# The opening of an attention and feed-forward kernel: the first root by logarithm and Newton step, three squares on VectorE, one copy moved

## Chip, core and metric

The kernel runs on one core of a Trainium2 chip. The metric is the time of one execution on the device in microseconds (us). Time before: 1337.54 us, the median of 3 runs (1336.25 to 1338.61). A core has a matrix engine (TensorE, PE in the profile), three engines for element-wise work (VectorE or DVE, ScalarE or ACT, GpSimd or POOL), and an engine (SP) that here does nothing but send transfers between main memory and the on-chip memory. Every engine takes its own instructions in order; they wait for one another through semaphores.

## What is computed

```python
def _attn_ref(q, k, v, g_q, g_k):            # q, k, v: (8, 12, 448, 64)
    def rmsnorm(x, g):
        rms = np.sqrt(np.mean(x * x, axis=-1, keepdims=True) + 1e-06)
        return x / rms * g
    q_n, k_n = (rmsnorm(q, g_q), rmsnorm(k, g_k))
    scores = scale * np.matmul(q_n, k_n.transpose(0, 1, 3, 2))
    attn = softmax(scores)                   # row maximum taken off, 1e-9 added to the sum
    return np.matmul(attn, v)

def _moe_ref(x, w_in, w_out):                # x: (3584, 768), w_in: (768, 2048), w_out: (2048, 768)
    r = np.maximum(x @ w_in, 0.0)
    return (r * r) @ w_out
```

Attention's output, with the heads side by side, is the `x` of the second function. All of it is in float32.

## The kernel before

Two heads of one batch row make a *pair*; there are 48. Pairs 0 to 11 (`NAT` is 12) are done first and alone, in `attention_alone`; the pairs that follow are done beside the matrix products of the feed-forward part, which come in four spans by a Strassen-like scheme with seven products in place of eight. The order of the work in each engine is the order in which the program is written (`manual_schedule`): nothing is moved by a scheduler.

**The first pair.** `first_pair` sends the loads of pair 0 and 1 (SP's queue: q(0), the two gain vectors, k(0), q(1), k(1)), fills `mhalf` with -0.5 on POOL, and has PE run three idle products on a zeroed tile. Then `normalise_in_turn` makes the roots. In the text q(i) and k(i) are the query and key halves of pair i. For each half: ACT squares it (L333), DVE adds up in groups of 64 (L334) and makes mean plus 1e-6 (L335), POOL raises that to the power -0.5 (L336). After the root of q, DVE multiplies q by it (L339), and that is the copy which PE transposes. k is not scaled: its root goes into the exponentials as a factor (L828). `between` stands after q's power: the three DVE steps for a bound on the scores (L1604 to L1606) and the product of the gains (L373). PE transposes k(0) and q(0) (L385), ACT copies both out of the PSUM banks (L387, L389, the latter with the gain).

Then all engines load the bound and branch: small scores take `attention_then_ffn_bounded`, which needs no row maximum. This is the branch that runs.

**A pair in `attention_alone`.** The 448 keys of a pair are cut into four chunks (`NJ`). `scores(i, c)` has PE make two products (one for each head) into one of two PSUM tiles `sc` (L824), and ACT takes two exponentials out of it (L828). A third chunk's products thus wait for the exponentials of the first. `transpose(i, s, n)` transposes q or k of the next pair (L794) and copies it (L796 for k, L803, in `gain`, for q). `values` multiplies by v (L887), `total_of` makes the row sums (L912), `add_up` adds chunks of exponentials on DVE (L841), `finish` turns the sums into factors and writes `xT` on DVE (L930 to L936).

`norm(i)` normalises the pair two ahead. For i up to 2 it calls `normalise_in_turn`, both squares on ACT. From i = 3 on one square takes both halves (L731), and `roots` makes the root without POOL: ACT takes a logarithm (L742) and an exponential (L743, with a bias tile `rebias`), DVE makes a Newton step of three small instructions (L744 to L746), POOL scales q (L747).

**The weights.** Beside this the weights are prepared in steps, `prepare(t)` for block t, four ticks each. The steps that the text names: ACT's absolute value (`unsigned`, L594), DVE's clamp (L608) in the first tick; ACT's scaling of the low words (L611) and DVE's shift (L613) in the second; DVE's merge (L618) in the third; POOL's integer addition of block t-1 (`value`, L580) in the third and fourth; POOL's sums and differences (L588). SP's loads of the blocks (L545) are in `load_words`. Each `yield` of `attention_alone` is a turn u, and after it `weights(upto)` runs ticks until `upto` are done:

```python
for u, _ in enumerate(attention_alone()):
    weights(min(EARLY, 2 * u + 1, 4 + (EARLY - 4) * u // (4 * NAT - 7)))
```

`EARLY` is 48. Before, 1, 3, 5, 7 and 8 ticks are done after turns 0 to 4. Pair 0 has one turn, the pairs that follow have four.

**The order in pair 0** is: scores (0,0) and (0,1), transposes of k(1), scores (0,2) and (0,3), transposes of q(1), `add_up`, `norm(2)`, load of v(1), first half of the values, load of pair 3.

Of the kernel before, what the change touches and what calls it, by code (L numbers as in the profile page):

```python
# [325 lines left out]
        nc.sync.dma_start(dst[:, :, h], k[b, h0 + h].rearrange("(p j) d -> p j d", j=4))  # L326


def normalise_in_turn(nc, raw, sq, rstd, mhalf, between=lambda: None):

    SP, _, n = rstd.shape
    for s in range(2):
        nc.scalar.activation(sq[:, s], raw[:, s], AF.Square)  # L333
        nc.vector.tensor_reduce(rstd[:, s], sq[:, s].rearrange("p (n d) -> p n d", n=n), AX, ALU.add)  # L334
        nc.vector.tensor_scalar(rstd[:, s], rstd[:, s], float(n) / sq.shape[2], 1e-6, ALU.mult, ALU.add)  # L335
        nc.gpsimd.tensor_tensor(rstd[:, s], rstd[:, s], mhalf[:SP, 0:n], ALU.pow)  # L336
        if s == 0:
            between()
            nc.vector.tensor_tensor(sq[:, 0].rearrange("p (j h d) -> p h j d", j=n // 2, h=2),  # L339
                                    raw[:, 0].rearrange("p (h j d) -> p h j d", j=n // 2, h=2),  # L340
                                    rstd[:, 0].rearrange("p (h j) -> p h j ()", h=2)
                                    .to_broadcast([SP, 2, n // 2, sq.shape[2] // n]), ALU.mult)


def chunk_of(pt, s, j, n):
# [4 lines left out]
def first_pair(tc, q, k, g_q, g_k, held):  # L350

    nc = tc.nc
    qk, qkT, ident, mhalf, gains, rstd, bound = held
    D = q.shape[-1]
    S = q.shape[2]
    NJ = 4
    SP = S // NJ
    raw, sq = (places_of(qk, 0, n)[:SP] for n in range(2))
    load_q(nc, qk, q, 0)
    bound[0]()  # L360
    load_k(nc, qk, k, 0)
    for i, g in enumerate((g_q, g_k)):
        for h in range(2):
            nc.gpsimd.dma_start(gains[h * D:(h + 1) * D, i:i + 1], g.rearrange("(d o) -> d o", o=1))
    load_q(nc, qk, q, 1)
    load_k(nc, qk, k, 1)
    nc.gpsimd.memset(mhalf, -0.5)
    make_identity(nc, ident)


    def between():
        bound[1]()
        nc.vector.tensor_scalar(gains[:, 0:1], gains[:, 0:1], gains[:, 1:2], float(D) ** -0.5, ALU.mult, ALU.mult)  # L373

    with tc.tile_pool(name="ps_first", bufs=1, space=bass.MemoryType.PSUM) as ps_first:

        nc.vector.memset(qkT[:, 1], 0.0)
        idle = ps_first.tile([2 * D, S], F32, name="idle")
        for _ in range(3):
            nc.tensor.matmul(idle, qkT[:, 1, 0, 0:2 * D], qkT[:, 1, 1], start=True, stop=True)  # L380
        normalise_in_turn(nc, raw, sq, rstd, mhalf, between)
        for s, src in ((1, raw[:, 1]), (0, sq[:, 0])):
            pt = ps_first.tile([2 * D, S], F32, name=f"pt{s}")
            for j in range(NJ):
                nc.tensor.transpose(chunk_of(pt, s, j, NJ), src[:, j * 2 * D:(j + 1) * 2 * D], ident[:SP, :SP])  # L385
            if s:
                nc.scalar.copy(qkT[:, 0, s], pt)  # L387
            else:
                nc.scalar.activation(qkT[:, 0, s], pt, AF.Copy, scale=gains[:, 0:1])  # L389
# [3 lines left out]
def attention_then_ffn_bounded(  # L393
# [73 lines left out]
        turn[0] += n is None  # L467
        return ps_m.tile([P, S], F32, tag="mn"[turn[0] % 2 if n is None else n], name=name)

    qk, qkT, ident, mhalf, gains, rstd0, _ = held  # L470
    gT = consts.tile([P, NFC, 2 * S], F32, name="gT")
    xT = consts.tile([P, 2, NPAIR, S], F32, name="xT")
    xC = consts.tile([P, 3, HC, S], F32, name="xC")
# [247 lines left out]
    def norm(i):  # L721
        if i >= NAT:
            squares(i)
            norm_by_squares(i)
            return scale_by_squares(i)
        raw, sq = (places_of(qk, i, n)[:SP] for n in range(2))
        rstd = rstds[i] = small.tile([SP, 2, 2 * NJ], F32, tag="rstd", name="rstd", bufs=4)
        normed[i] = sq[:, 0], raw[:, 1]
        if i <= 2:
            return normalise_in_turn(nc, raw, sq, rstd, mhalf)  # L730
        nc.scalar.activation(sq, raw, AF.Square)  # L731
        nc.vector.tensor_reduce(rstd, sq.rearrange("p s (n d) -> p s n d", d=D), AX, ALU.add)
        nc.vector.tensor_scalar(rstd, rstd, 1.0 / D, 1e-6, ALU.mult, ALU.add)

    def roots(i):


        raw, sq = (places_of(qk, i, n)[:SP] for n in range(2))
        rstd = rstds[i]
        flat = rstd.rearrange("p s n -> p (s n)")  # L740
        y, t = (small.tile([P, 2 * S // 32], F32, tag=tag, name=tag)[:SP, 0:4 * NJ] for tag in ("half", "other"))
        nc.scalar.activation(y, flat, AF.Ln, scale=2.0 ** -63)  # L742
        nc.scalar.activation(y, y, AF.Exp, scale=-0.5, bias=sums["rebias"])  # L743
        nc.vector.scalar_tensor_tensor(t, y, -0.5, flat, ALU.mult, ALU.mult)  # L744
        nc.vector.tensor_tensor(t, t, y, ALU.mult)
        nc.vector.scalar_tensor_tensor(flat, t, 1.5, y, ALU.add, ALU.mult)  # L746
        nc.gpsimd.tensor_tensor(sq[:, 0].rearrange("p (j h d) -> p h j d", j=NJ, h=2),  # L747
                                raw[:, 0].rearrange("p (h j d) -> p h j d", j=NJ, h=2),
                                rstd[:, 0].rearrange("p (h j) -> p h j ()", h=2).to_broadcast([SP, 2, NJ, D]),
                                ALU.mult)  # L750
# [36 lines left out]
    def transpose(i, s, n):  # L787

        if n is None:
            pt = bank("pt", 1) if i % 2 == 0 else ps_o.tile([P, S], F32, tag="o", name="pt")  # L790
        else:
            pt = bank("pt", n)
        for j in range(NJ):
            nc.tensor.transpose(chunk_of(pt, s, j, NJ), normed[i][s][:, j * P:(j + 1) * P], ident[:SP, :SP])  # L794
        if s:
            nc.scalar.copy(qkT[:, i % 2, s], pt)  # L796
        elif n is None:
            turned[i] = pt
        else:
            gain(i, pt)  # L800
# [1 line left out]
    def gain(i, pt):  # L802
        nc.scalar.activation(qkT[:, i % 2, 0], pt, AF.Copy, scale=gains[:, 0:1])  # L803

    def scores(i, c):


        if i >= NAT:
            sc = ps_s.tile([P, 2, 512], F32, tag="s", name="sc")
            n = S if c < NF else S // 2  # L810
            for h in range(2):
                rows = slice(h * D, (h + 1) * D)
                for m, part in enumerate(sides):
                    keys = slice(c * P + m * D, c * P + (m + 1) * D) if c < NF else slice(NF * P, S)
                    of = slice(0, S) if c < NF else slice(m * n, (m + 1) * n)
                    nc.tensor.matmul(sc[part, h, 0:n], qkT[rows, 0, 1, keys], qkT[rows, 0, 0, of], start=True, stop=True)  # L816
            pr = probs[i, c] = places[(NF * i + c) % len(places)] if c < NF else halves[i % 2]
            nc.scalar.activation(pr, sc[:, :, 0:n], AF.Exp)  # L818
            return
        at = i % 2  # L820
        sc = ps_s.tile([SP, 2, 512], F32, tag="s", name="sc")
        for h in range(2):
            rows = slice(h * D, (h + 1) * D)
            nc.tensor.matmul(sc[:, h, 0:S], qkT[rows, at, 1, c * SP:(c + 1) * SP], qkT[rows, at, 0, :],  # L824
                             start=True, stop=True)
        pr = probs[i, c] = places[(NJ * i + c) % len(places)][:SP]
        for h in range(2):
            nc.scalar.activation(pr[:, h], sc[:, h, 0:S], AF.Exp, scale=rstds[i][:, 1, 2 * c + h:2 * c + h + 1])  # L828
# [124 lines left out]
    def attention_alone():  # L953


        for i in range(NAT):
# [5 lines left out]
            if i == 0:  # L962

                transpose(1, 1, 1)
                scores(0, 2)
                scores(0, 3)
                transpose(1, 0, 0)
                add_up(0, 1)
                norm(2)
                load_v(1)  # L970
                values(0, (0, 1))
                load(3)
                yield
                continue
# [524 lines left out]
    with tc.tile_pool(name="words", bufs=2) as spare["pool"]:  # L1499
# [5 lines left out]
        with tc.tile_pool(name="first", bufs=2, reuse_waits="tile") as work:  # L1505
# [4 lines left out]
            sums["turned"], sums["factors"] = (g[:, 0:S] for g in free[2 * NJ + 2:2 * NJ + 4])  # L1510
            sums["ones"] = work.tile([SP, D], F32, tag="ones", name="ones", bufs=1)
            nc.vector.memset(sums["ones"], 1.0)
            sums["rebias"] = work.tile([SP, 1], F32, tag="rebias", name="rebias", bufs=1)
            nc.vector.memset(sums["rebias"], -31.5 * math.log(2.0))
            for u, _ in enumerate(attention_alone()):

                weights(min(EARLY, 2 * u + 1, 4 + (EARLY - 4) * u // (4 * NAT - 7)))
                if u == 4 * NAT - 9:
                    load_blocks(5)
        with tc.tile_pool(name="first_product", bufs=2, reuse_waits="tile") as work:  # L1520
# [54 lines left out]
def kernel(  # L1575
# [27 lines left out]
    def square_of_bound():  # L1603
        nc.vector.tensor_tensor(gg[:, 0, :], gg[:, 0, :], gg[:, 1, :], ALU.mult)  # L1604
        nc.vector.tensor_tensor(gg[:, 0, :], gg[:, 0, :], gg[:, 0, :], ALU.mult)
        nc.vector.tensor_reduce(top, gg[:, 0, :], AX, ALU.max)  # L1606

    held = (
        bound.tile([128, 8, 8 * D], F32, name="qk"),
        bound.tile([128, 2, 2, S], F32, name="qkT"),  # L1610
        bound.tile([128, 128], F32, name="ident"),
        bound.tile([128, 2 * (S // 32)], F32, name="mhalf"),
        bound.tile([128, 2], F32, name="gains"),
        bound.tile([S // 4, 2, 8], F32, name="rstd0"),
        (load_gains, square_of_bound),
    )
    with tc.manual_schedule():
# [42 lines left out]
```

## Time and profile before

| what | value |
|---|---|
| median of 3 runs | 1337.54 us (1336.25 to 1338.61) |
| the profiled execution, its own time | 1336.47 us |
| its span, from first to last instruction | 1334.6 us |
| PE busy | 1319.8 us (99%) |
| DVE, ACT, POOL busy | 856.0, 486.4, 678.7 us |
| DVE, ACT, POOL busy from 0 to 20 us | 9.68, 14.65, 12.11 us |
| PE busy from 0 to 20 us, from 20 to 57, from 57 to 60, from 60 to 127 | 16.63, 36.14, 2.65, 66.16 us |
| clock granted to PE | 1.00 in all stretches of the opening |

The page puts 93% of the chain that ended last on PE. A busy time near the length of a stretch means that the engine sets the pace there or is close to it. In a timeline each line has its start, its duration, the engine, the line of the program, the operation and its operands with their shapes; `qk<-qk` names the tile written and the tile read. Idle time before an instruction stands in brackets, with the last work that ended before it; a wait for several things is put down to the one that came last by the profile.

### The profile page before, as it was taken

What the parts mean: (1) busy time and instruction counts of PE and PEld (TensorE: products, weight loads), DVE (VectorE), ACT (ScalarE), POOL (GpSimd) and SP (SyncE); (2) the same over time, 40 slices, a digit from 0 to 9 for tenths busy, and PEclk for the clock granted to TensorE, in tenths of its full rate; (3) what the DMA queues carried; (4) which work ended last, traced back from release to release, by engine and by line L of the source; (5) the groups of instructions that cost most, each with busy time, mean ns of one, the idle gap of its engine ahead of it and who ended that gap; (6) DMA issues with size and microseconds to landing.
All of it is one profiled execution on the core that took longest, in us unless ns stands there. A gap on an engine that the chain in (4) does not pass through costs nothing.

```text
span 1334.6 us, 17767 instructions
## 1 busy us (share of the span) xinstructions
PE 1319.8 (99%) x5930; PEld 699.0 (52%) x5930; DVE 856.0 (64%) x1334; ACT 486.4 (36%) x939; POOL 678.7 (51%) x544
## 2 busy tenths in 40 slices
PE   8999999999999999999999999999999999999997
PEld 3334454444446654444444755444444665557887
DVE  6999898589987233467887523457888723336553
ACT  8885656555540012255542011235554001111000
POOL 5677444467756123566774322448775622322452
PEclk9999999999999999999999999999999999999999
DMA  8787999656664333356656433345764444321433
GB/s 233 217 219 197 361 384 324 188 125 133 138 152 117 85 89 88 99 115 140 132 130 144 100 98 89 99 109 111 140 134 126 114 90 153 115 87 48 116 106 55
DMA packets 413817, 190.18 MB, mean 142 GB/s; under 512 B 282388, under 2 KB 408724, under 8 KB 413716
## 3 DMA queue, kind: packets, MB, share of 16 engines
q1 hardware_dynamic: 406164, 180.21, 51.7%
q0 software_dynamic: 4736, 8.40, 2.5%
q8 instruction: 49, 0.80, 0.3%
q10 hardware_dynamic: 2816, 0.34, 0.2%
q14 instruction: 52, 0.43, 0.1%
HBM read 155.72 MB, written 33.16 MB: 142 GB/s over the span
## 4 chain that ended last, share of the span: by engine, by line
PE 93%; DVE 3%; ACT 2%; issue 1%; DMA 1%; POOL 0%; SPq 0%; ACTq 0%
PE ps L1217 21%; PE pd L1117 11%; PE pa L1117 10%; PE pc L1117 10%; PE sc L816 7%; PE pav L898 7%; PE pb L1117 5%; PE ps L1400 3%; PE ps L1268 3%; PE pd L1372 2%; PE pc L1372 2%; PE pa L1372 2%; PE sc L824 2%; PE pav L887 2%; PE pd L1202 1%; PE pa L1202 1%
## 5 line engine op out<-in xcount | busy, mean ns | idle before, releaser
L1089 POOL TENSOR_TENSOR gT<-gT 128x448 f32<-128x448 f32 x96 | 93.7, 978 | 258.5 <-ACT gT L1085 258.5
L773 POOL TENSOR_TENSOR half<-half,mhalf 128x28 f32<-128x28 f32 x36 | 184.7, 5131 | 68.2 <-DVE half L772 46.0
L1217 PE MATMUL ps<-gT,sw 128*128 128x448 f32 x432 | 169.3, 545 | 0.0
L1085 ACT ACTIVATE gT<-gT 128x448 f32<-128x448 f32 x96 | 55.3, 576 | 293.7 <-DVE gT L1133 293.6
L1117 PE MATMUL pa<-xT,sw 128*128 128x448 f32 x384 | 154.9, 539 | 0.0
L1217 PEld LDWEIGHTS ps<-gT,sw 128*128 128x128 f32 x432 | 80.1, 190 | 87.1 <-issue 85.3
L1217 PE MATMUL ps<-gC,sw 128*128 128x448 f32 x288 | 113.1, 546 | 0.0
L816 PE MATMUL sc<-qkT 64*64 64x448 f32 (+1 forms) x1152 | 110.0, 497 | 0.3 <-ACT pr L818 0.2
L1117 PEld LDWEIGHTS pa<-xT,sw 128*128 128x128 f32 x384 | 72.8, 190 | 70.7 <-issue 70.7
L588 POOL TENSOR_TENSOR gC<-gC 128x384 f32<-128x384 f32 x64 | 72.1, 1144 | 60.2 <-DVE gC L584 58.5
L1217 PEld LDWEIGHTS ps<-gC,sw 128*128 128x128 f32 x288 | 53.3, 190 | 59.5 <-issue 58.2
L866 POOL DMA_DIRECT2D xT<-factors x72 | 38.0, 532 | 90.9 <-DMA factors<-square 59.0
L1133 DVE TENSOR_TENSOR gT<-z,pd 128x448 f32<-128x448 f32 x32 | 19.9, 621 | 99.1 <-PE pd L1117 98.9
L818 ACT ACTIVATE pr<-sc 128x896 f32<-128x896 f32 x87 | 76.9, 908 | 12.0 <-PE sc L816 11.8
L775 POOL TENSOR_TENSOR qk<-qk,half 128x448 f32<-128x448 f32 x72 | 76.7, 1085 | 2.8
L1117 PE MATMUL pd<-xT,sw 128*128 128x448 f32 x192 | 77.8, 541 | 0.2
L1117 PE MATMUL pd<-xC,sw 128*128 128x448 f32 x192 | 77.5, 540 | 0.0
L1117 PE MATMUL pc<-xC,sw 128*128 128x448 f32 x192 | 77.5, 540 | 0.0
L1117 PE MATMUL pc<-xT,sw 128*128 128x448 f32 x192 | 77.4, 539 | 0.0
L1117 PE MATMUL pb<-xC,sw 128*128 128x448 f32 x192 | 77.4, 539 | 0.0
L898 PE MATMUL pav<-pr,vt 64*64 64x448 f32 x348 | 72.7, 537 | 0.0
L898 PE MATMUL rest<-pr,vt 64*64 64x448 f32 x348 | 72.7, 537 | 0.0
(282 smaller groups left out, 2447.6 us busy)
## 6 DMA issues: line engine op xcount, KB each, us to landing
sw<-w1s SPq DMA_DIRECT2D x224, 192.0 KB, 2.4
sw<-w2s SPq DMA_DIRECT2D x102, 256.0 KB, 3.4
w1s<-gC SPq DMA_DIRECT2D x8, 1344.0 KB, 7.3
w2s<-gC SPq DMA_DIRECT2D x8, 1344.0 KB, 6.3
qk<-in_q_dram SPq DMA_DIRECT2D x144, 56.0 KB, 2.5
qk<-in_k_dram SPq DMA_DIRECT2D x144, 56.0 KB, 2.5
xT<-factors POOLq DMA_DIRECT2D x72, 112.0 KB, 3.5
words<-in_moe_w_out_dram SPq DMA_DIRECT2D x9, 768.0 KB, 7.5
```

Source lines behind the costliest of these rows:

```text
L588: nc.gpsimd.tensor_tensor(*[blocks_of(n)[:, place_of(n, i)] for i in (dst, x, y)], op)
L773: nc.gpsimd.tensor_tensor(half, half, mhalf, ALU.pow)
L775: nc.gpsimd.tensor_tensor(qkn[:, s], raw[:, s], half[:, s * NG:(s + 1) * NG].rearrange("p g -> p g ()").to_broadcast([P, NG, 32]), ALU.mult)
L816: nc.tensor.matmul(sc[part, h, 0:n], qkT[rows, 0, 1, keys], qkT[rows, 0, 0, of], start=True, stop=True)
L818: nc.scalar.activation(pr, sc[:, :, 0:n], AF.Exp)
L898: nc.tensor.matmul(into, vs[i][rows, h, c, :], probs[i, c][rows, h, :], start=(c == 0), stop=(c == NF), skip_group_check=True)
L1085: nc.scalar.activation(g, src, AF.Relu)
L1089: nc.gpsimd.tensor_tensor(g, g, g, ALU.mult)
L1117: nc.tensor.matmul(ps, stream[n + at][:, c], rhs[:, c], start=first and c == 0, stop=c == HC - 1, skip_group_check=not first)
L1217: nc.tensor.matmul(ps, stream[n][:, c % 4], rhs_of[i][:, c], start=c == 0, stop=c == HF - 1)
L1268: nc.tensor.matmul(ps, stream[n][:, c % 4], rhs_of[i][:, c], start=c == 0, stop=c == HF - 1)
L1372: nc.tensor.matmul(ps, lhs[:, c], rhs[:, c], start=first and c == 0, stop=c == HK - 1, skip_group_check=not first)
```

## The change

Five things are done.

1. The root of q(0) is no longer a power on POOL. ACT takes a logarithm and an exponential (`first_root`), DVE makes one Newton step (`newton`); the small tiles that they need lie in `sq`. The three steps for the bound stand between the two, the product of the gains behind the scaling of q(0). The bias tile `rebias` is made at the very start, in one tile with `mhalf`; `roots` uses the same two functions and the same tile.
2. In pair 1 the square of k, in pair 2 the squares of q and k are products on DVE (`by_vector`).
3. In pairs 1 and 2 the mean and the power of k come before the scaling of q.
4. The transposes and the copy of q(1) are issued inside `scores(0, 3)`, between its products and its exponentials. PE's order stays as it was; ACT's copy of q(1) now stands ahead of the two exponentials of (0,3).
5. `2 * u + 1` becomes `2 * u`: 0, 2, 4, 6 and 8 ticks are done after turns 0 to 4, and from turn 4 on the count is the same as before.

```diff
+def newton(nc, y, t, x):
+
+    nc.vector.scalar_tensor_tensor(t, y, -0.5, x, ALU.mult, ALU.mult)
+    nc.vector.tensor_tensor(t, t, y, ALU.mult)
+    nc.vector.scalar_tensor_tensor(x, t, 1.5, y, ALU.add, ALU.mult)
+
+
+def first_root(nc, y, x, rebias):
+
+    nc.scalar.activation(y, x, AF.Ln, scale=2.0 ** -63)
+    nc.scalar.activation(y, y, AF.Exp, scale=-0.5, bias=rebias)
+
+
+def normalise_in_turn(nc, raw, sq, rstd, mhalf, between=None, rebias=None, by_vector=()):
 
     SP, _, n = rstd.shape
-    for s in range(2):
-        nc.scalar.activation(sq[:, s], raw[:, s], AF.Square)
+
+    def means(s):
+        if s in by_vector:
+            nc.vector.tensor_tensor(sq[:, s], raw[:, s], raw[:, s], ALU.mult)
+        else:
+            nc.scalar.activation(sq[:, s], raw[:, s], AF.Square)
         nc.vector.tensor_reduce(rstd[:, s], sq[:, s].rearrange("p (n d) -> p n d", n=n), AX, ALU.add)
         nc.vector.tensor_scalar(rstd[:, s], rstd[:, s], float(n) / sq.shape[2], 1e-6, ALU.mult, ALU.add)
+
+    def power(s):
         nc.gpsimd.tensor_tensor(rstd[:, s], rstd[:, s], mhalf[:SP, 0:n], ALU.pow)
-        if s == 0:
-            between()
...
+    means(0)
+    if between:
+        y, t = sq[:, 0, 0:n], sq[:, 0, n:2 * n]
+        first_root(nc, y, rstd[:, 0], rebias)
+        between[0]()
+        newton(nc, y, t, rstd[:, 0])
+        scaled()
+        between[1]()
+    else:
+        power(0)
+    means(1)
+    power(1)
+    if not between:
+        scaled()
...
+        nc.vector.memset(rebias, -31.5 * math.log(2.0))
         nc.vector.memset(qkT[:, 1], 0.0)
...
-        normalise_in_turn(nc, raw, sq, rstd, mhalf, between)
+        normalise_in_turn(nc, raw, sq, rstd, mhalf, (bound[1], gain), rebias)
...
         if i <= 2:
-            return normalise_in_turn(nc, raw, sq, rstd, mhalf)
+            return normalise_in_turn(nc, raw, sq, rstd, mhalf, by_vector=(1,) if i == 1 else (0, 1))
...
-    def scores(i, c):
+    def scores(i, c, between=None):
...
+        if between:
+            between(1, 0, 0)
         pr = probs[i, c] = places[(NJ * i + c) % len(places)][:SP]
...
                 scores(0, 2)
-                scores(0, 3)
-                transpose(1, 0, 0)
+                scores(0, 3, transpose)
...
-                weights(min(EARLY, 2 * u + 1, 4 + (EARLY - 4) * u // (4 * NAT - 7)))
+                weights(min(EARLY, 2 * u, 4 + (EARLY - 4) * u // (4 * NAT - 7)))
...
+    powers = bound.tile([128, 2 * (S // 32) + 1], F32, name="mhalf")
     held = (
...
-        bound.tile([128, 2 * (S // 32)], F32, name="mhalf"),
+        powers[:, 0:2 * (S // 32)],
...
+        powers[:S // 4, 2 * (S // 32):],
         (load_gains, square_of_bound),
```

`scaled()` is the product that L339 makes before; `gain` in the first pair is the product of L373.

## The prediction

> **What bounds the kernel now.** First come the waits of TensorE (PE) over the whole span (who waited for whom, us in total, times, longest):
>
> ```profile
> PE idle L380 <- DVE qkT L377: 1.9, 1, 1.9
> PE pt L794 <- DVE xT L936: 1.2, 1, 1.2
> PE sc L824 <- ACT gT L828: 0.8, 2, 0.6
> PE sc L824 <- ACT qkT L389: 0.8, 1, 0.8
> PE pt L794 <- ACT qkT L796: 0.3, 1, 0.3
> ...
> ```
>
> Then busy times in stretches of the opening (length; PE, weight loads, DVE, ACT, POOL; clock, DMA share, GB/s):
>
> ```profile
> 15.00:20.00 5.00, 4.67 (x28) 1.88 (x24) 2.40 (x6) 4.76 (x10) 2.82 (x3) 1.00 0.85 203
> 20.00:30.00 10.00, 10.00 (x55) 3.90 (x53) 9.73 (x17) 9.77 (x18) 4.96 (x4) 1.00 0.95 291
> 30.00:43.00 13.00, 13.00 (x70) 5.13 (x70) 12.30 (x22) 12.50 (x23) 6.70 (x6) 1.00 1.13 270
> ```
>
> Then the timelines of POOL, DVE and ACT (start, duration; in brackets idle time before and what ended it), and the landing of k(3)'s load (last figure: us from issue):
>
> ```profile
> 10.44 1.64 POOL L336 TENSOR_TENSOR rstd<-rstd,mhalf 112x8 f32<-112x8 f32 x1 [0.57 <-DVE rstd L335]
> 13.68 2.49 POOL L336 TENSOR_TENSOR rstd<-rstd,mhalf 112x8 f32<-112x8 f32 x1 [1.60 <-DVE rebias L1514]
> ```
>
> ```profile
> 19.82 0.55 DVE L608 TENSOR_SCALAR gC<-gC 128x768 f32<-128x768 f32 x1
> 20.29 1.09 DVE L841 TENSOR_TENSOR gT<-gT 112x896 f32<-112x896 f32 x1
> ...
> 26.69 0.63 DVE L936 TENSOR_TENSOR xT<-pav,gT 128x448 f32<-128x448 f32 x1
> 27.23 1.19 DVE L613 TENSOR_SCALAR gC<-gC 128x768 uint32<-128x768 uint32 x1
> ```
>
> ```profile
> 18.94 0.64 ACT L796 COPY qkT<-pt 128x448 f32<-128x448 f32 x1
> 19.82 1.06 ACT L731 ACTIVATE qk<-qk 112x1024 f32<-112x1024 f32 x1 [0.24 <-DVE rstd L334]
> ...
> 23.38 0.31 ACT L743 ACTIVATE half<-half,rebias 112x16 f32<-112x16 f32 x1
> 23.59 0.91 ACT L594 ACTIVATE gC<-gT 128x768 f32<-128x768 f32 x1
> 24.41 1.14 ACT L828 ACTIVATE gT<-sc,rstd 112x448 f32<-112x448 f32 x2
> ...
> 32.80 0.21 ACT L742 ACTIVATE half<-rstd 112x16 f32<-112x16 f32 x1 [0.28 <-DVE rstd L733]
> ```
>
> ```profile
> qk<-in_k_dram SPq DMA_DIRECT2D x2, 112.0 KB, 5.9
> ```
>
> To be seen: after 19.63 us PE waits about 2.2 us in all (the second and third line and one of 0.2), the rest before; so the end moves by as much as PE's place after the opening does. But in 20 to 43 us PE (23.0 of 23.0 us) has ScalarE (ACT, 22.3) and VectorE (DVE, 22.0) right beside it. Before 20 us both have room: DVE is busy 2.40 of the 5 us from 15 on. What leaves the early stretch for the later one costs nearly its full length there.
>
> **The change, part by part.** Numbers in brackets such as (1,0) are pair and chunk.
>
> *First root.* Out: GpSimd's (POOL) power of q(0), 4.94 to 6.62, which releases the scaling of q(0) at 6.65. In: Ln and Exp (0.21 and 0.31 in the rows at 23.14 and 23.38, there on 16 columns, here on 8) and three DVE steps that start 0.21 apart. From the mean's end at 4.86: Ln 4.90 to 5.11, Exp 5.15 to 5.46, steps 5.49 to 6.08, scaling 6.12 instead of 6.65. The three bound steps (4.77 to 5.48) fit under Ln and Exp. The gain factor, which waited for its load until 6.34, goes behind the scaling; left ahead of it, it would have held it to 6.55. k(0) is the rival for PE: its transposes run from 6.50 to 7.17, so q(0)'s start at about 7.1 instead of 7.49, and its copy, behind k(0)'s copy (7.20 to 7.73), at 7.77 instead of 8.10: 0.33. The first exponentials wait for k(0)'s power as well (8.22, behind a mean that waited for DVE's scaling); with DVE free its reduction follows the square (end 6.99) at 7.03, the power is at about 8.0, and they start at 9.75 instead of 9.97: 0.22. The new 0.06 us memset ahead of qkT's is covered by PE's idle matmuls. No other table load: the two functions already run between exponentials at L742 and L743, with the one load at 0.73.
>
> *Squares of k(1), q(2), k(2)* leave ACT (two took 1.15) for DVE, 0.69 each by the scaling at 12.11 (L339, same elements, two inputs). DVE's gaps of 1.32, 1.75, 1.10 and 1.75 us between 9 and 18.4 us hold these 2.07 us. Price: k(1)'s square stands at about 9.9 to 10.6, just when q(1)'s power starts (10.05). The power that met a two-input DVE step (13.68) took 2.49 instead of 1.64, so it ends between 11.7 and 12.2; before, 12.08. I take the upper end, as the row is the same pair of operations: q(1) gains nothing. k(1)'s mean is now ahead of q(1)'s scaling; its power ends by about 14.4 instead of 16.17, with nothing on the path waiting for it.
>
> *q(1)'s copy ahead of exponentials (0,3).* q(1)'s transposes stay at about 13.17, the copy follows at 13.8 instead of 14.54; queued behind it are exponentials (0,3), delayed to 14.4. PE's value products still begin at 13.70, so scores (1,0) stay at about 15.36. Exponentials (1,0) need both heads' scores, 1.06 us after their start (the distance from 44.74 to 45.80): 16.4 instead of 16.87, since two squares and L594 are out of the way. k(2)'s copy ends at about 19.1 instead of 19.58, and q(2)'s transposes start when PE is free, 19.30: **PE gains 0.33 us at 19.63.** Had q(1) come earlier, this would be 0.5.
>
> *The weights' steps* run one tick later in the first four turns. SP's order of transfers does not change by it, nor POOL's; what moves is L594 and L608 of block 0, then L618, L608 and L613. Walk on from k(3): sent at 13.42 and 14.04, 5.9 us to landing, about 19.3 to 19.9, so ACT's square of pair 3 at 19.82 is held by the load whatever the row names. The transfers before it leave at most 0.4 us sooner: 19.45 to 19.82. Then L594, which used a gap at 16.09 (0.97), stands in front of L611, q(2)'s copy, exponentials (1,2), Ln and Exp; a slot of it costs 0.83 (23.59 to 24.41). So the Exp that ended at 23.69 ends at 24.15 to 24.5. DVE's Newton steps wait for it (24.19 to 24.55 instead of 24.09), after an idle of 1 to 2 us, and L618 (0.96), which ran before them, runs after: the transpose at 25.06 goes to 25.57 at best (+0.5). Behind xT (L936), L608 (0.55) now precedes L613. Without POOL in the way both end at 28.75, against 28.42 before (+0.33). But L613 took 1.19 instead of 0.55 beside L580 (26.01 to 28.01), and L618 now overlaps L747's start, which pushes L580 to about 26.8 to 28.8: then they end at about 29.8 (+1.4). The rest (two sums, L618, the reduction) follows at the old durations.
>
> So Ln of pair 4, which already waited for DVE at 32.80, comes x = 0.33 to 1.4 later, and with it exponentials (2,3) (34.07 to 35.21). They free the bank of the second half of the scores at 34.88, that is 35.76: slack 0.45 with 0.1 for the release. PE's shift is the larger of -0.33 and x - 0.45: -0.12 to +0.95. I take x = 1.0, nearer the contended end because the L613 row is the same step beside the same POOL work: **+0.55 us**. At 43.35 DVE had 0.38 idle, so it is late by 0.62 there, PE by 0.55; the 1.2 us wait at 57.35 moves with both, and after 68 us DVE waits for PE's products again, so nothing more is lost or won.
>
> Sum: profiled execution 1336.47 (span 1334.6 and 1.87 around it) + 0.55 = 1337.0; it lies 1.07 under the median of the three runs, so for the median 1337.54 + 0.55 = **1338.1**.
>
> The Trainium skill speaks against the change more strongly: "SBUF — State Buffer", section "Who interferes with whom", says that a DVE instruction with two SBUF inputs and a GpSimd instruction that reads SBUF exclude each other for the whole instruction, whichever is issued first. This trace agrees for POOL (the 2.49), but not for DVE beside a power: the sum at 20.29 took its usual 1.09 inside a power of 19.99 to 21.87. By the row the scaling of q(1) passes beside k(1)'s power; by the rule it waits for it, and the sum would be that of the second rival.
>
> **The rivals.** *The front's gain is kept:* k(3) lands early, POOL misses L608 and L613, x stays under 0.45; 0.33 to 0.5 is won: 1337.1. For it: SP sends q(2) and k(2) earlier. Against: DVE and ACT 97% and 98% busy from 20 to 30 us, into which 1.5 us of work is moved.
>
> *Slower by the shared port:* k(1)'s power now stands right behind q(1)'s on POOL. If it holds DVE's scaling of q(1) for its 1.64, scaling goes from 12.11 to 13.75, transposes to 14.5; queued behind them on PE are value products (15.1) and scores (1,0) (16.7, +1.35), behind the copy on ACT exponentials (0,3) and (1,0) (+0.9). q(2)'s transposes go to 20.65 (+1.0), pair 3's square to 20.4, and with L594's 0.83 x becomes about 2.2: PE +1.75, 1339.3. It decides as soon as the scaling starts after the power. Against: the 1.09 row.
>
> *It does nothing:* k(0)'s power, not q(0)'s, sets the first exponentials, and the 0.45 slack takes x: 1337.5.
>
> **How the numbers follow.** Forecast 0.48, gain kept 0.28, port 0.14, nothing 0.10. Systematic ends are -0.5 and +1.75; the three runs lie 2.4 us apart, so a median may be off by some 0.8. Range 1336.2 to 1339.8; the forecast's own is 1337.2 to 1339.0. A change of 0.2%, 2.7 us, is about what a measurement of this kernel tells from none. Faster by that much needs nearly all of the 3.4 us in which PE stands before 20 us: 0.04. Slower by that much is the port's rival met again at q(2): 0.12. Else 0.84.
>
> **What would show it.** Right: scaling of q(0) near 6.12; PE's transposes of q(2) near 19.3 without a wait; Newton's steps of pair 3 after an idle DVE; L608 and L613 behind the first xT beside L580; a PE wait for exponentials near 35.7. Wrong: q(1)'s scaling over a microsecond after its power's end (port); no PE wait near 36 and the xT wait before 57.2 (gain kept); new waits of PE past 60 us, where I expect none.

## The result, and the profile after

The changed kernel takes 1339.19 us (median of 19 runs, 1337.74 to 1341.86), the kernel before on the same chip 1337.35 us (19 runs, 1336.05 to 1338.61). The ratio is 1.0016, with a 95% interval of 1.0009 to 1.0023: slower by 1.84 us (by the interval 1.2 to 3.1). That is less than the 0.2%, or 2.7 us, that the prediction called no measurable change, but the interval excludes a ratio of 1. The forecast was 1338.1, slower too, with 1337.2 to 1339.0 as its own range and 1336.2 to 1339.8 over all cases. The profiled execution after took 1338.28 us, with a span of 1336.4.

Lines of the changed kernel have new numbers. Those that matter, old to new: L594 is L628, L608 is L642, L611 is L645, L613 is L647, L618 is L652, L580 is L614, L731 is L765, L742/743 are L338/339, L744 to 746 are L331 to 333, L794 is L825, L824 is L855, L828 is L861, L588 is L622, L747 is L778, L930/936 are L963/969, L841 is L874.

First the waits of PE in the changed kernel (who waited for whom, us in total, times, longest):

```profile
PE idle L414 <- DVE qkT L411: 1.9, 1, 1.9
PE pt L825 <- DVE xT L969: 1.8, 2, 1.4
PE sc L855 <- ACT gT L861: 1.4, 4, 0.6
PE pc L1149 <- DMA sw<-w1s: 0.9, 2, 0.5
PE sc L855 <- ACT qkT L423: 0.8, 1, 0.8
PE pt L419 <- DMA qk<-in_k_dram: 0.7, 1, 0.7
```

Against before: the wait for xT has a second place (1.8 instead of 1.2), that for the exponentials two more (1.4 instead of 0.8), and a wait for the first product's weights is new in this list. The last line is k(0)'s load, before 7 us. The busy times in the same three stretches (length; PE, weight loads, DVE, ACT, POOL; clock, DMA share, GB/s):

```profile
15.00:20.00 5.00, 5.00 (x28) 2.18 (x28) 3.56 (x7) 3.29 (x7) 3.64 (x2) 1.00 0.97 221
20.00:30.00 10.00, 9.60 (x52) 3.52 (x48) 7.77 (x15) 9.97 (x18) 3.50 (x3) 1.00 0.96 289
30.00:43.00 13.00, 12.76 (x66) 4.62 (x64) 12.59 (x19) 11.63 (x22) 6.44 (x5) 1.00 1.12 232
```

Before 20 us ACT has got room (3.29 instead of 4.76) and PE is filled. Behind it PE, which had no gap from 20 to 43 us, has one of 0.40 and one of 0.24, and DVE idles for 2.2 us of the ten from 20 on (0.3 before), which pushes its work behind 30 us. An engine that idles in a crowded stretch is waiting for its neighbour. The timelines of DVE and ACT show for what (start, duration; in brackets idle time before and what ended it):

```profile
6.25 0.69 DVE L358 TENSOR_TENSOR qk<-qk,rstd 112x512 f32<-112x512 f32 x1
...
12.09 0.69 DVE L358 TENSOR_TENSOR qk<-qk,rstd 112x512 f32<-112x512 f32 x1 [0.61 <-POOL rstd L355]
...
24.44 0.17 DVE L331 SCALAR_TENSOR_TENSOR other<-half,rstd 112x16 f32<-112x16 f32 x1 [1.13 <-ACT half L339]
...
24.95 0.95 DVE L652 SCALAR_TENSOR_TENSOR gC<-gC 128x768 uint32<-128x768 uint32 x1
25.82 0.64 DVE L963 STREAM_TRANSPOSE gT<-tot 128x448 f32<-128x448 f32 x1
...
27.45 0.62 DVE L969 TENSOR_TENSOR xT<-pav,gT 128x448 f32<-128x448 f32 x1
27.99 1.20 DVE L642 TENSOR_SCALAR gC<-gC 128x768 f32<-128x768 f32 x1
```

```profile
19.73 1.06 ACT L765 ACTIVATE qk<-qk 112x1024 f32<-112x1024 f32 x1 [0.73 <-DVE gT L874]
20.70 0.90 ACT L628 ACTIVATE gC<-gC 128x768 f32<-128x768 f32 x1
21.48 0.93 ACT L645 ACTIVATE gC<-gC 128x768 int32<-128x768 uint32 x1
...
24.10 0.31 ACT L339 ACTIVATE half<-half,mhalf 112x16 f32<-112x16 f32 x1
...
34.04 0.22 ACT L338 ACTIVATE half<-rstd 112x16 f32<-112x16 f32 x1 [1.12 <-DVE rstd L767]
```

The square of pair 3 starts at 19.73, with ACT idle for 0.73 us ahead of it: ACT was ready sooner and gained nothing. Directly behind it now stands the absolute value of block 0 (L628), which before ran in a gap at 16.09. The Exp ends 0.72 later than before (24.41 against 23.69), Newton's steps wait for it, the merge L652 follows them instead of going ahead, the transpose starts at 25.82 instead of 25.06, and the logarithm of pair 4 at 34.04 instead of 32.80. On PE that gives these two new waits:

```profile
28.22 0.57 PE L825 MATMUL pt<-ident,qk 112*128 112x112 f32 x4 [0.36 <-DVE xT L969]
...
36.48 1.01 PE L855 MATMUL sc<-qkT 64*112 64x448 f32 x4 [0.24 <-ACT gT L861]
```

Matching the matrix instructions of both profiles one by one gives PE's place against before: -0.50 us at q(2)'s transposes, -0.29 at 26.3, +0.32 at 28.2, +0.76 at 36.5, +1.01 at 38.0, +1.22 at 58.6 (57.35 before), +2.57 at 212, +2.65 at the last product; the span grows by 1.8 only, as the end behind the last product is shorter.

### The profile page after: what moved, and what is told of

Read it like the earlier page. It is cut to its first block, busy times and chain, and to the rows that moved or that the text cites. A ratio compares the mean times of both kernels' runs of the same rounds, so it can differ in the third digit from the quotient of the medians.

```text
span 1336.4 us, 17767 instructions
## 1 busy us (share of the span) xinstructions
PE 1320.4 (99%) x5930; PEld 698.4 (52%) x5930; DVE 859.7 (64%) x1340; ACT 485.2 (36%) x938; POOL 679.8 (51%) x543
## 4 chain that ended last, share of the span: by engine, by line
PE 90%; DVE 4%; ACT 2%; DMA 2%; issue 1%; POOL 1%; SPq 0%; POOLq 0%; ACTq 0%; DVEq 0%
PE ps L1249 21%; PE pd L1149 10%; PE pc L1149 10%; PE pa L1149 10%; PE sc L847 7%; PE pav L931 7%; PE pb L1149 5%; PE ps L1432 3%; PE ps L1300 3%; PE pd L1404 2%; PE pc L1404 2%; PE pa L1404 2%; PE pd L1234 1%; PE pa L1234 1%; PE pc L1234 1%; PE sc L855 1%
## 5 line engine op out<-in xcount | busy, mean ns | idle before, releaser
L622 POOL TENSOR_TENSOR gC<-gC 128x384 f32<-128x384 f32 x64 | 72.3, 1146 | 61.4 <-DVE gC L618 59.7
L1157 DVE TENSOR_TENSOR z<-p,pb 128x448 f32<-128x448 f32 x32 | 19.8, 619 | 82.3 <-PE pb L1149 79.3
```

What stands on the lines that cost most here:

```text
L622: nc.gpsimd.tensor_tensor(*[blocks_of(n)[:, place_of(n, i)] for i in (dst, x, y)], op)
```

## The experiments

Twelve runs were made: nine edited kernels, and three repeats (e7, e8, e11). Each is set against the kernel before that ran beside it. Three figures sum up each profile: when the square of pair 3 starts (this is where a late k(3) shows), when the logarithm of pair 4 starts, and PE's place at the wait for xT, at 57.35 us in the first profile of before. "Distance" is the second figure less the first.

| kernel | square of pair 3 | Ln of pair 4 | distance | PE at 57 us | ratio to before, 95% interval |
|---|---|---|---|---|---|
| before | 19.82 | 32.80 | 12.98 | 0 | |
| before, again (e8) | 19.62 | 32.90 | 13.28 | +0.52 | 0.9996 [0.9987, 1.0005] |
| old ticks (e1) | 19.52 | 32.43 | 12.91 | -0.39 | 1.0004 [0.9995, 1.0013] |
| old ticks, again (e11) | 20.48 | 33.41 | 12.93 | +0.58 | 1.0008 [0.9999, 1.0017] |
| old ticks, k(3) sent sooner (e6) | 19.00 | 32.14 | 13.14 | -0.51 | 1.0004 [0.9995, 1.0013] |
| first root alone (e10) | 20.31 | 33.57 | 13.26 | +0.93 | 1.0002 [0.9993, 1.0011] |
| absolute value at its old place (e5) | 19.90 | 33.38 | 13.48 | +0.57 | 1.0009 [1.0000, 1.0018] |
| absolute value alone late (e9) | 20.39 | 34.12 | 13.73 | +1.29 | 1.0008 [0.9999, 1.0017] |
| changed kernel | 19.73 | 34.04 | 14.31 | +1.22 | 1.0016 [1.0009, 1.0023] |
| changed kernel, again (e7) | 20.42 | 34.72 | 14.30 | +1.88 | 1.0012 [1.0002, 1.0021] |
| squares back on ACT (e3) | 21.28 | 35.60 | 14.32 | +2.79 | 1.0008 [0.9999, 1.0017] |
| copy back (e4) | 20.11 | 34.43 | 14.32 | +1.61 | 1.0013 [1.0004, 1.0023] |
| new ticks alone (e2) | 20.38 | 34.71 | 14.33 | +1.91 | 1.0009 [1.0000, 1.0018] |
| changed, k(3) sent sooner (e12) | 18.75 | 33.06 | 14.31 | +0.23 | 1.0002 [0.9993, 1.0011] |

The times alone hardly tell single kernels apart, since their intervals overlap; in groups they do. By medians, the kernels with all the moved steps and the old order of loads are 1.3 to 2.0 us slower than the kernel before beside them (changed, e7, e2, e3, e4), those with a part of the moved steps 0.8 and 0.9 (e9, e5), those with the old ticks 0.1 to 0.5 (e1, e11, e6, e10), and e12 is 0.2 slower.

**The weights' steps at their old ticks (e1).** The changed kernel with

```diff
-                weights(min(EARLY, 2 * u, 4 + (EARLY - 4) * u // (4 * NAT - 7)))
+                weights(min(EARLY, 2 * u + 1, 4 + (EARLY - 4) * u // (4 * NAT - 7)))
```

> The changed kernel with the weights' steps where they were (2u + 1 ticks after turn u); all else as changed. Moved-step theory: ACT's absolute value of block 0 falls into ACT's wait of 0.98 us before exponentials (1,0) and costs nothing there, Exp of pair 3 ends near 23.6 instead of 24.4, DVE has no wait of 1.1 us before its Newton step, L613-type shifts stay ahead of POOL's additions, and PE keeps its 0.5 us of 19.1 us through 57 us: PE's first product at 57 us about 0.4 to 0.5 earlier than before (near 56.9), total 0.9997 of before, about 1336.9. Squares-or-port theory (three squares on VectorE collide with GpSimd and cost the time): 57 us stays 1.0 or more later than before, ratio 1.0010 or more.

Measured: PE's lead of 0.65 at q(2)'s transposes is still 0.39 at 57 us, and the distance is 12.91. ACT's timeline of this run shows the square held by the load, and no absolute value behind it:

```profile
19.52 1.06 ACT L765 ACTIVATE qk<-qk 112x1024 f32<-112x1024 f32 x1 [0.67 <-DMA qk<-in_k_dram]
20.48 0.90 ACT L645 ACTIVATE gC<-gC 128x768 int32<-128x768 uint32 x1
```

So the moved steps cause the loss in the opening. The time, though, does not come out under the kernel before (1338.24 us, ratio 1.0004; some 1336.9 had been expected).

**The new ticks alone (e2),** in the kernel before: the same line, `2 * u + 1` to `2 * u`.

> The kernel before with nothing but the weights' steps one tick later (2u). Moved-step theory: pair 3's square still starts at 19.8, Exp of pair 3 ends 0.8 later (24.5), the reduction of pair 4 on DVE 1.2 to 1.4 later, a PE wait of 0.8 to 0.95 for exponentials (2,3) near 36, at 57 us PE is 1.0 to 1.3 later; ratio 1.0008 to 1.0016. Squares-or-port theory and copy theory: nothing lost, ratio 1.0000 within the interval.

Measured: distance 14.33, PE +1.91. In that execution PE was 1.07 behind at q(2)'s transposes already, by a fall of its clock (last section), and the square of pair 3 came 0.56 later than in the first profile of before; the moved steps add the other 1.35. The time is 1.0009, with an interval that just reaches 1.

**Squares (e3) and copy (e4) undone,** each in the changed kernel:

```diff
-            return normalise_in_turn(nc, raw, sq, rstd, mhalf, by_vector=(1,) if i == 1 else (0, 1))
+            return normalise_in_turn(nc, raw, sq, rstd, mhalf)
```

```diff
-                scores(0, 3, transpose)
+                scores(0, 3)
+                transpose(1, 0, 0)
```

> The changed kernel with the squares of k(1), q(2), k(2) back on ScalarE. Moved-step theory: ACT takes k(1)'s square in its wait of 0.90 before exponentials (0,0) and the two others in its wait of 0.98 before (1,0); at 57 us PE is as late as in the changed kernel, 1.2 (1.0 to 1.5) after before; ratio 1.0008 to 1.0016. Squares-or-port theory: the loss goes, ratio under 1.0004.

> The changed kernel with q(1)'s transposes and copy after the exponentials of (0,3), as before. Moved-step theory: q(1)'s copy goes from 13.7 to about 14.6, scores (1,0) from 15.26 to about 15.35, the 1.1 us of room before pair 3's square takes the rest; at 57 us PE is 1.2 (1.0 to 1.4) after before; ratio 1.0008 to 1.0016. Copy theory (the copy ahead of the exponentials holds ACT up and costs the time): ratio under 1.0004.

Measured: neither gives the loss back. The distance is 14.32 in both, as in the changed kernel; PE stands later than there (+2.79 and +1.61), because k(3) came later. This is the square in the run of e3:

```profile
21.28 1.06 ACT L765 ACTIVATE qk<-qk 112x1024 f32<-112x1024 f32 x1 [2.37 <-DMA qk<-in_k_dram]
```

Neither the squares on DVE nor the copy is the loss. The mean and the power of k ahead of the scaling of q, which the second rival needs, are still in place in e3 and e4; but e1 has them too, without the loss, and e2 has the loss without them.

**Only the absolute value of block 0 at its old place (e5).** In the changed kernel `prepare(0)` gives way once behind its absolute value, and one step more is taken in all:

```diff
+            yield
...
-        while taken[0] < upto:
+        while taken[0] < upto + 1:
```

> The changed kernel with ACT's absolute value of block 0 alone back after turn 0; every other step of the weights as late as in the changed kernel. Moved-step theory in two halves: ACT's slot of 0.8 us is one, DVE's order (merge behind the Newton step, clamp behind the first xT beside POOL) the other. Then Exp of pair 3 ends about 0.8 earlier than in the changed kernel (near 23.6), pair 4's logarithm 0.4 after before instead of 1.2, and PE at 57 us 0 to 0.3 after before. If ACT's slot were all of it: 0.4 earlier than before. If DVE's order were all of it: 1.2 later, as in the changed kernel.

Measured: distance 13.48 instead of 14.31, and the transpose at 25.18 instead of 25.82. PE at 57 us is +0.57, more than the 0 to 0.3 expected. DVE's timeline of this run shows what is left:

```profile
24.31 0.95 DVE L653 SCALAR_TENSOR_TENSOR gC<-gC 128x768 uint32<-128x768 uint32 x1
25.18 0.64 DVE L964 STREAM_TRANSPOSE gT<-tot 128x448 f32<-128x448 f32 x1
```

The merge (here L653) is still behind Newton's steps, and the clamp behind xT.

**Only the absolute value late (e9),** the complement: `2 * u + (u > 0)`, which makes 0, 3, 5, 7 ticks.

> The changed kernel with one part of the moved steps kept: ScalarE's absolute value of block 0 stays a turn late, all later steps stand where they stood before the change. Theory of two parts (the absolute value's slot on ScalarE, and VectorE's order around Newton's steps and the first xT): Exp of pair 3 ends near 24.4 and Newton's steps start behind it at 24.4, as in the changed kernel, but the clamp L642 is ahead of the transpose again, which then starts near 25.3 (25.82 changed, 25.06 before); Ln of pair 4 at 32.9 to 33.2 (34.04 changed); no wait of PE for xT near 28; PE's shift at 57 us -0.3 to +0.3, some 1.0 less than the changed kernel's +1.22. Rival, the absolute value is the whole loss: transpose 25.8, Ln of pair 4 near 34, PE's shift +1.2 as in the changed kernel.

Measured: the numbers of the expectation were missed, because k(3) came late again (square at 20.39, idle 1.48 before it); both theories had taken 19.7. The distance is 13.73. The clamp of block 0 stands in the same tick and is late with the absolute value (22.82, 18.04 in e1), but it runs ahead of Newton's steps, which then wait 0.16 for ACT's Exp: here ACT sets the pace. Against 12.93 with the old ticks (e11, a square at nearly the same time) the absolute value costs 0.80; the other steps by themselves (e5) 13.48 - 12.93 = 0.55. Together 1.35; measured together 14.31 - 12.93 = 1.38. The loss thus has two parts that add up, and neither is the whole.

**The second weight block sent behind k(3) (e6),** in e1's kernel. SP's queue holds two weight blocks of 768 KB ahead of q(3) and k(3); one of them is sent behind:

```diff
                 load(3)
+                load_w(loaded[0])
+                loaded[0] += 1
...
-        for _ in range(2):
-            load_w(loaded[0])
-            loaded[0] += 1
+        load_w(loaded[0])
+        loaded[0] += 1
```

> The first experiment (all of the change but the weights' steps) with the load of weight block 1 sent after pair 3's loads instead of before. Load theory: k(3) lands near 17 instead of 19.5, pair 3's square starts at 18.8 behind k(2)'s copy with no wait, Exp of pair 3 ends near 22.5, block 1 lands near 20, in time; PE at 57 us 0.4 to 0.7 earlier than before, ratio 0.9992 to 1.0000. Rival (the square waits for VectorE, not for the load): it starts at 19.5 as in the first experiment and nothing moves.

Measured: the square starts at 19.00 without a wait, and PE stands at -0.51. The time still does not come out under the kernel before (1.0004; 0.9992 to 1.0000 had been expected). What was won is partly lost where ACT then waits for a weight block:

```profile
26.26 0.93 ACT L628 ACTIVATE gC<-gT 128x768 f32<-128x768 f32 x1 [0.69 <-DMA gT<-in_moe_w_in_dram]
```

**The changed kernel and the kernel before, again (e7, e8).**

> The changed kernel once more. Moved-step theory: again DVE idle near 1.1 us before pair 3's Newton step, PE waits for the exponentials near 36 and is 1.0 to 1.6 late at 57 us; if k(3) lands later than 19.7, more. If the loss of the first profile was chance, under 0.4 at 57 us. Waits of PE for weights near 170 to 210 us come again if the change makes them, and not if they are chance.

> The kernel before once more, to see how far two profiles of one program lie apart: ratio 1.0000 within the interval; PE at 19 us and at 57 us within 0.3 of the first profile if the opening repeats, up to 1 off if PE's clock or k(3)'s landing varies.

Measured: the changed kernel is slower again, 1.0012 [1.0002, 1.0021], the kernel before the same as itself. The profiles of both differ from their first ones, at 57 us by 0.66 and 0.52 and at the last product by 3.7 and 2.3, more than the effect itself. PE's waits in the second profile of before include

```profile
PE pd L1202 <- DVE pr L1284: 0.7, 2, 0.4
PE pa L1117 <- DMA sw<-w1s: 0.4, 1, 0.4
...
PE pav L887 <- DMA vt<-in_v_dram: 0.3, 1, 0.3
```

and PE's place in it, against the first profile, is +0.52 at 57 us and +2.29 at the last product. The waits past 60 us that looked new in the changed kernel thus come and go in the unchanged one. At the last product every one of the thirteen other profiles is behind the first profile of before, by 0.7 to 6.3 us, in no order that fits their places at 57 us: that first profile was of a quick execution (1336.47 us, where the 19 runs have 1336.05 to 1338.61). In the second profile of the changed kernel PE loses 2.6 us in one wait for POOL near 420 us, where the others have 1.1 at most.

**The first root alone (e10),** that is e1's kernel with e3's and e4's edits.

> The kernel before with the first root alone: squares on ScalarE, q(1)'s copy behind exponentials (0,3), the weights' steps as before the change. Theory that the first root makes the opening's gain: first exponentials near 9.85, PE at q(2)'s transposes -0.3 to -0.5 against before, and about -0.4 kept at 57 us, as k(3)'s landing (19.4 to 19.7) is what the squares and the copy run into anyway; time 0.2 to 0.6 us under the kernel before. Rival, the squares and the copy carry half of the gain: PE only -0.1 to -0.2 at q(2)'s transposes.

Measured: the first root brings the opening forward as expected up to scores (0,3) (-0.46 at q(0)'s transposes, -0.15 from 11 us on), but at q(2)'s transposes only -0.14 of it is left, where the kernels with squares and copy have -0.43 to -0.65: the rival's number. Then k(3) came late (20.31), PE at 57 us is +0.93 instead of -0.4, and the time is that of the kernel before. What the front has won at 11 us differs from run to run (0.10 to 0.32). From there to q(2)'s transposes PE wins another 0.40 in the changed kernel and in e1, 0.40 with the squares and without the copy (e4), 0.11 with the copy and without the squares (e3), and nothing here: the squares carry most of PE's lead at 19 us, since they free ACT.

**The old ticks again (e11).**

> The changed kernel with the weights' steps at their old ticks, repeated. Theory: PE -0.4 to -0.65 at 57 us again, time 0.3 to 0.7 us under the kernel before, so 1336.9 to 1337.4 beside its 1337.6, and under the changed kernel by 1.5 to 2. Rival, the opening's gain is given back after 60 us: the time is 0.5 us above the kernel before again, as in its first run, and PE's later waits for weights' loads or VectorE's products are longer than those of the kernel before.

Measured: PE at 57 us is +0.58, not -0.4 to -0.65, and the time 1.0008 [0.9999, 1.0017]. The distance repeats to 0.02 (12.93), but not the start of the square:

```profile
20.48 1.06 ACT L765 ACTIVATE qk<-qk 112x1024 f32<-112x1024 f32 x1 [1.59 <-DMA qk<-in_k_dram]
```

ACT idles for 1.59 us here, with the opening's lead of 0.61 in hand. The lead reaches the square only if k(3) has landed.

**The changed kernel with e6's order of loads (e12).**

> The changed kernel with its moved steps, and only the second weight block's load sent behind k(3)'s. Theory of two terms: PE's shift at 57 us is the delay of the square of pair 3 against 19.82 (set by k(3)'s landing) plus 1.3 for the moved steps (1.28 to 1.35 in five profiles so far). With the load in front the square starts at 19.0 without a wait, so Ln of pair 4 at about 33.3 and PE +0.5 (up to +0.9, as in the earlier kernel with this load order the second block's late landing took 0.3); the time about 0.7 to 1.3 us under the changed kernel's. Rival, the landing decides nothing: PE +1.2 to +1.9 at 57 us as in the changed kernel.

Measured: square at 18.75 without a wait, distance 14.31, Ln of pair 4 at 33.06, PE +0.23. By the two terms: 18.75 - 19.82 + 1.30 = +0.23. The time is 1337.74 us beside 1337.54 of the kernel before, ratio 1.0002 [0.9993, 1.0011], where the changed kernel had 1.0016 and 1.0012. ACT's timeline of this run:

```profile
18.75 1.10 ACT L765 ACTIVATE qk<-qk 112x1024 f32<-112x1024 f32 x1
19.71 0.93 ACT L628 ACTIVATE gC<-gC 128x768 f32<-128x768 f32 x1
...
33.06 0.22 ACT L338 ACTIVATE half<-rstd 112x16 f32<-112x16 f32 x1 [1.03 <-DVE rstd L767]
```

and DVE's timeline of it:

```profile
18.50 1.09 DVE L874 TENSOR_TENSOR gT<-gT 112x896 f32<-112x896 f32 x1 [0.38 <-ACT gT L861]
```

The sum L874 is named as what released the square in the changed kernel (19.73). Here the square runs while this sum is still at work, so it does not need it. That leaves the load as what ended last in the changed kernel too.

With the load out of the way the front's lead does arrive and pays for most of the moved steps in this one profile. None of the kernels is measurably faster than the kernel before.

## Why the prediction came out as it did

These rows, in each fence first of before and then of the changed kernel, belong to the step that failed:

```profile
43.35 0.65 DVE L930 STREAM_TRANSPOSE gT<-tot 128x448 f32<-128x448 f32 x1 [0.38 <-PE tot L912]
45.54 1.08 DVE L618 SCALAR_TENSOR_TENSOR gC<-words,gC 128x768 uint32<-128x768 uint32 x1
...
44.39 0.65 DVE L963 STREAM_TRANSPOSE gT<-tot 128x448 f32<-128x448 f32 x1 [0.17 <-PE tot L945]
46.57 1.29 DVE L652 SCALAR_TENSOR_TENSOR gC<-words,gC 128x768 uint32<-128x768 uint32 x1
```

```profile
43.84 1.97 POOL L588 TENSOR_TENSOR gC<-gC 128x384 f32<-128x384 f32 x2
...
45.08 1.97 POOL L622 TENSOR_TENSOR gC<-gC 128x384 f32<-128x384 f32 x2
```

- **Scaling of q(0) at 6.12, first exponentials at 9.75.** Measured 6.25 and 9.87: right to 0.13; in this execution ACT's first square already started at 3.42, 0.12 later than before.
- **The power of q(1) stretched beside k(1)'s square, q(1) gains nothing.** Right: the scaling starts at 12.09, against 12.11 before. With the squares back on ACT (e3) the two powers took 3.24 us and it started at 11.83.
- **The port rival.** Its test was whether the scaling of q(1) is held by k(1)'s power. POOL was at its two powers from 10.04 to 13.66 (3.62 us, where two alone take 3.28), and the scaling started at 12.09 and ran in its usual 0.69 us. The rival fell with this row. That its total, 1339.3, lies nearer to the measured 1339.19 than the forecast does is chance.
- **PE's lead of 0.33 at q(2)'s transposes.** Measured 0.50, with exponentials (1,0) at 16.37 as forecast (16.4). By e10, e3 and e4 it is mostly the squares off ACT that bring it (0.40 of it), less the first root (0.10); the size was off by 0.17.
- **k(3)'s landing holds the square of pair 3, "19.45 to 19.82".** The mechanism was right and turned out to be the main one: in all nine profiles with the new front and the old order of loads ACT idles ahead of this square, for 0.67 to 2.37 us, and in seven of them the load is named. The bounds were too narrow: 19.5 to 21.3.
- **The moved steps delay the logarithm of pair 4 by x, taken as 1.0 of 0.33 to 1.4.** Both parts (ACT's slot, DVE's order) were right, with 0.80 for the slot (0.83 taken) and 0.55 for the order. The contended end came true: the clamp beside POOL's additions took 1.20, and clamp and shift ended at 29.79, where 29.8 was said for that end. In the changed kernel x was 1.24, so 1.0 was too little; from the square on it is 1.32 to 1.40 against 12.98, 12.91 and 12.93, and 1.03 against the second profile of before (13.28), where ACT also waited 0.82 for a weight block.
- **"PE's shift is the larger of -0.33 and x - 0.45".** This is the step that failed. At 36.5 us it holds: 1.24 - 0.45 = 0.79, measured +0.76. But it left out the bank that xT is read from: PE waits for it at 28.2, and at 38.01, again 0.15 us behind the end of an xT, it is later by another 0.16.
- **"At 43.35 DVE had 0.38 idle, so it is late by 0.62 there."** The other half of the step that failed: these 0.38 us took up nothing. DVE waits there for PE's sums, which were late themselves: 0.17 was left, and the transpose came 1.04 late. The merge behind it (L618, now L652) then took 1.29 us instead of 1.08 and ended 1.24 late, just as POOL's two sums beside it did. In all fourteen profiles this merge ends 0.81 or 0.82 us behind the end of POOL's sums, and idle time and merge together take 1.45 or 1.46 us, however they share it. POOL's sums follow its scaling of q, and this waits for Newton's steps; so x comes to DVE by way of POOL, past the idle time. (Whether a port or a tile ties the merge to POOL, no run shows.) The xT of 56.58 came at 57.80, 1.22 late, and PE pays all of x at 57 us: +1.22, not +0.55. Of the 0.67 between them about 0.24 is x and 0.45 the slack. In the table PE's place at 57 us agrees with the delay of Ln of pair 4 to 0.05 us in the changed kernel and in nine of the twelve experiments; the three that differ, by 0.15 to 0.42, have another wait in between: e6 and e8 ACT's for a weight block (0.69 and 0.82), e10 one of 0.96 on PE for the first xT. With the logarithm of pair 5 (41.31 before) PE's place agrees to 0.05 in all thirteen.
- **Nothing past 60 us.** The first profile spoke against it (+1.4 there), the second profile of before takes this back: it has +1.8 there without any change. Single profiles can't carry this question.

The forecast case came true with a term that was too small by 0.67 us: 1337.54 + 1.22 would have been 1338.8, and the measured 1339.19 is 0.4 from that (0.6 by the 1337.35 of the same measurement), inside what the runs spread. The range's upper end does not follow from its own terms, 1337.54 + 1.75 + 0.8 = 1340.1; the measured time lies inside either. "Gain kept" and "it does nothing" fell with the waits at 28.2 and 36.5 us, which e1 does not have.

What stays open: whether the new front itself makes k(3) land later. From issue to landing its load took 5.6 to 5.9 us in three profiles with the old front and 5.7 to 7.7 in nine with the new one and the same order of loads, though it was sent at 12.8 to 13.5 us instead of 13.4 to 13.6. In all of them the transfers share the stretch of 13 to 16 us at 340 to 370 GB/s, with a DMA share near 1.1, so sending sooner into it has little to win. Three profiles are too few to call the difference an effect, and if it is one, it would explain only in part why the kernels with the old ticks are not faster than before: in e6 the load holds nothing and PE is 0.51 ahead at 57 us, yet its time is 1.0004 of before. Where such a lead goes past 60 us, no run shows. Nor is it shown that the opening makes all of the 1.84 us: the two profiles of the changed kernel have 1.22 and 1.88 at 57 us, the two of before 0 and 0.52.

## What to carry to other kernels

A lead won on one engine is worth what the next fixed point lets through: find the landing that the lead runs into (here a load queued behind two weight blocks) before adding it up. A step taken out of a gap of a half-idle stretch and put into a stretch where two engines are full costs its whole slot plus what it does to the order behind it, 0.8 and 0.55 us here. Slack found in a timeline counts only if what ends it is not late as well; an idle time that waits for the delayed engine is no slack, nor is one behind which another engine brings in the same delay.

## What the runs showed of the hardware

**The granted clock fell once to a half in the opening.** In the profile of e2 PE waited for 0.71 and 0.77 us between 6.9 and 9.0 us (0.33 and 0.77 in the first profile of before). These are its busy times in three stretches, in the order of columns used above:

```profile
6.00:9.00 3.00, 1.51 (x9) 0.79 (x9) 1.68 (x4) 1.88 (x4) 1.39 (x2) 1.00 0.73 176
9.00:13.00 4.00, 3.98 (x14) 1.83 (x16) 1.57 (x4) 3.07 (x6) 2.69 (x2) 0.57 0.87 227
13.00:20.00 7.00, 7.00 (x38) 2.90 (x40) 2.81 (x8) 6.62 (x14) 4.13 (x2) 1.00 0.91 252
```

PE was busy for half of the first stretch, the clock granted in the second was 0.57 (0.50 from 9.31 to 12.72 us, 1.00 before and behind), and eight passes of scores took 3.09 us instead of 1.76. This cost 1.07 us at q(2)'s transposes. The Trainium skill, page "TensorE: Matmul & The Clock Gate", section "Part 1: The HAM clock gate (the "warmup" mystery)", gives half speed as the idle state, entered after an idle window of about 3.4 us. Here PE, once started at 1.85 us, stood idle for no longer than 0.77 us at a time, and the other profiles, with PE busy for 1.66 us or more of the same 3 us, kept 1.00. So a window without work is not needed for the fall; what is, no run shows.

**A load's landing was less steady than the engines behind it.** The distance of the table repeats to 0.03 us over six profiles of five kernels (14.30 to 14.33), and in the two of before, one with a longer wait for a weight block, to 0.30 (12.98 and 13.28). The landing of k(3), behind the same two blocks, moved from 18.9 to 20.7 us over twelve profiles.
